# Another order of all pieces in a fused linear-attention and feed-forward kernel

## The chip, the cores and the metric

The kernel runs on 1 core of one Trainium2 chip. The metric is the device time of the program in microseconds (us), the median of three runs. Beside the timed runs there is one execution taken by the hardware profiler; all rows below are of that one.

## The reference

Two stages. The first is a gated linear attention with 4 batches, 8 heads, 768 tokens, head width 32 and 16 states, in fp32. With `cum` the running sum of `log(a)` in a chunk, per head:

```python
L = np.exp(cum[:, :, :, None] - cum[:, :, None, :]) * causal
y_intra = ((Cc @ Bc.T) * L) @ xc
y_inter = (Cc @ state) * np.exp(cum)
state = decay_full * state + sum_j(Bc[j] * decay_from_j[j] * xc[j])
```

The second takes the 256 numbers of a token (8 heads of 32), normalizes them and adds a feed-forward block of hidden width 1024:

```python
xn = (x - mu) / np.sqrt(var + 1e-06) * g_ln
out = x + np.maximum(xn @ w_ch1, 0.0) @ w_ch2
```

The weights arrive as float64 and the inputs as fp32; the matmuls of the feed-forward block are each done on a rounded upper part and on a rest (names ending in h and l), so that three products stand for one.

## The kernel before

**Tiling.** The 768 tokens are six chunks `t` of 128; a chunk is handled for all 4 batches at once (512 columns). In a chunk the attention runs as: decays (`lr`, `dc`, `du`, `x`), scaled inputs `cs`, `cm`, `bs`, `be`; scores `G` (L394, 64 TensorE instructions); `R` = G times the decay table `WW` (L400, four on VectorE); state products `Z` (L433); `K`, `S`, `sbd`, the state between half chunks; `Vi` (L413), what the state gives, and `V` (L421), what the chunk gives, both into PSUM tiles `yps`; `y` copies them to `y32`. Then `yh`, `yl` split them, `T` (L482) transposes them, `tc`, `st`, `ag`, `rs`, `rc` make the statistics of each token.

**Feed-forward.** `h t m` (L513) makes one eighth of the hidden layer in 6 matmuls of 512 columns; `hh` and `hl` (L518/L520, L524) split it; `o t b` (L531) makes the output of one batch in 24 matmuls of 256 columns, `oc` (L541) does the same in pieces of 12 for chunk 0 as the second weights arrive; `oe` (L546) finishes it and `od` stores it. PSUM has 3 buffers for `h` and `o` (a buffer is free when its `hl` or `oe` is done) and 5 for the attention.

**Weights.** Each 512 KB piece of a weight is loaded (`ld w1 c k`, `ld w2 c`) and turned from float64 to fp32 by `k0`, `k1`, `k2`, `k3`, `kr`, `f` (L195, L200, L209, L214, L220, L225). The first weights are then centred: `wc` (L240) on TensorE for half 1, and `wm`, `wf` (L245, L249) for half 0; `wh` and `wl` (L254, L258) split them.

**Order.** There is no scheduler at work: the string `ISSUE` (L584) lists some 640 pieces, each a name with its arguments, and the loop at L577 issues them as they stand. A suffix gives the engine (`:v` VectorE, `:a` ScalarE, `:p` GpSimd). So each engine's instructions run in the order in which the string names them, and each waits for what it reads. `fill` pieces (L558) are matmuls on zeros that nobody reads. `pc` (L171) is a one-element transfer out of a loaded tile: SyncE's queue, which issues all transfers, stops there until that load has landed. A transfer also waits for the transfer eight before it, since eight semaphores are used in turn.

Of the kernel before, what the change touches and what calls it, by code (L numbers as in the profile page):

```python
# [659 lines left out]
```

## Time and profile before

| | |
|---|---|
| three timed runs | 196.64, 197.25, 197.37 us; median 197.25 us |
| profiled execution, its own time | 198.06 us |
| its span (first to last instruction) | 196.3 us |
| mean granted clock of TensorE | 0.981 |
| busy: TensorE matmul, weight load | 187.3 us (95%), 160.3 us (82%) |
| busy: VectorE, ScalarE, GpSimd | 131.0 us (67%), 67.0 us (34%), 38.3 us (20%) |
| chain that ended last | 89% TensorE |

The profiled execution lies 0.81 us above the median, and 1.76 us of it lie outside the span. The page names engines PE (TensorE matmul), PEld (its weight loads), DVE (VectorE), ACT (ScalarE), POOL (GpSimd) and SP (SyncE). A matmul on fp32 operands that isn't a transpose shows as two matmul and two weight-load instructions, one on the split operands as one of each. "Issue" is idle time for which the profile shows no releaser.

### The profile page before, as it was taken

What the parts mean: (1) busy time and instruction counts of PE and PEld (TensorE: products, weight loads), DVE (VectorE), ACT (ScalarE), POOL (GpSimd) and SP (SyncE); (2) the same over time, 40 slices, a digit from 0 to 9 for tenths busy, and PEclk for the clock granted to TensorE, in tenths of its full rate; (3) what the DMA queues carried; (4) which work ended last, traced back from release to release, by engine and by line L of the source; (5) the groups of instructions that cost most, each with busy time, mean ns of one, the idle gap of its engine ahead of it and who ended that gap; (6) DMA issues with size and microseconds to landing.
All of it is one profiled execution on the core that took longest, in us unless ns stands there. A gap on an engine that the chain in (4) does not pass through costs nothing.

```text
span 196.3 us, 6366 instructions
## 1 busy us (share of the span) xinstructions
PE 187.3 (95%) x2834; PEld 160.3 (82%) x2834; DVE 131.0 (67%) x278; ACT 67.0 (34%) x128; POOL 38.3 (20%) x40
## 2 busy tenths in 40 slices
PE   8785999999999999998999999999999999999993
PEld 3664557788899897998878799988999899998993
DVE  2499558999997899585897662496452791447210
ACT  4474598887234502015123540223102030014100
POOL 0043076904543740006420000000000002000000
PEclk9998599999999999999999999999999999999999
DMA  4896894040655033404000500200020001000024
GB/s 139 310 387 233 306 329 161 5 115 0 212 168 164 0 107 102 116 28 140 27 5 3 165 0 13 70 0 3 27 80 3 3 0 58 0 20 6 28 84 134
DMA packets 11670, 18.43 MB, mean 94 GB/s; under 512 B 2394, under 2 KB 5882, under 8 KB 11642
## 3 DMA queue, kind: packets, MB, share of 16 engines
q1 hardware_dynamic: 11642, 18.02, 27.9%
q8 instruction: 22, 0.36, 0.7%
q14 instruction: 6, 0.05, 0.1%
HBM read 14.74 MB, written 3.28 MB: 92 GB/s over the span
## 4 chain that ended last, share of the span: by engine, by line
PE 89%; DMA 3%; DVE 3%; issue 2%; ACT 1%; SPq 1%
PE ph L513 34%; PE po L531 29%; PE pp L541 6%; PE yps L421 5%; PE yps L413 3%; PE yt L482 3%; DMA raw<-in_w_dram 3%; PE G L394 3%; PE wc L240 3%; PE Z L433 2%; DVE o L546 1%; PE wm L245 1%; SPq L164 1%; DVE WW L382 1%; DVE bs L364 0%
## 5 line engine op out<-in xcount | busy, mean ns | idle before, releaser
L531 PE MATMUL po<-w,hh 128*128 128x256 f32 x320 | 56.9, 280 | 0.0
L513 PE MATMUL ph<-yh,w 128*128 128x512 f32 x192 | 53.8, 401 | 0.5 <-issue 0.5
L531 PEld LDWEIGHTS po<-w,hh 128*128 128x128 f32 x320 | 49.3, 188 | 1.5 <-issue 0.7
L531 PE MATMUL po<-w,hl 128*128 128x256 f32 x160 | 44.7, 279 | 0.6 <-issue 0.6
L513 PEld LDWEIGHTS ph<-yh,w 128*128 128x128 f32 x192 | 34.3, 188 | 7.8 <-issue 1.3
L518 ACT ACTIVATE hh<-ph 128x512 fp32r<-128x512 f32 x32 | 18.8, 598 | 57.7 <-PE ph L513 41.2
L524 DVE SCALAR_TENSOR_TENSOR hl<-ph,hh 128x512 fp32r<-128x512 f32 x48 | 32.4, 681 | 8.5 <-ACT hh L518 8.2
L531 PEld LDWEIGHTS po<-w,hl 128*128 128x128 f32 x160 | 30.1, 188 | 0.0
L513 PE MATMUL ph<-yl,w 128*128 128x512 f32 x96 | 29.8, 391 | 0.0
L546 DVE SCALAR_TENSOR_TENSOR o<-po,rstd,ytok 128x256 f32<-128x256 f32 x20 | 9.5, 480 | 26.5 <-PE po L531 26.3
L513 PEld LDWEIGHTS ph<-yl,w 128*128 128x128 f32 x96 | 18.0, 188 | 4.0
L474 POOL TENSOR_TENSOR yl<-y,yh 128x512 fp32r<-128x512 f32 x5 | 7.1, 1423 | 63.9 <-ACT yh L471 62.0
L400 DVE TENSOR_TENSOR R<-G,WW 128x512 f32<-128x512 f32 x24 | 15.5, 676 | 0.8 <-PE G L394 0.8
L520 DVE TENSOR_SCALAR hh<-ph 128x512 fp32r<-128x512 f32 x16 | 10.9, 684 | 7.1 <-PE ph L513 7.0
L421 PE MATMUL yps<-R,xt 64*32 64x64 f32 x768 | 9.8, 239 | 1.8 <-issue 1.8
L541 PE MATMUL pp<-w,hh 128*128 128x256 f32 x64 | 11.4, 280 | 0.0
L421 PEld LDWEIGHTS yps<-R,xt 64*32 64x32 f32 x768 | 8.6, 111 | 2.6 <-issue 2.3
L541 PEld LDWEIGHTS pp<-w,hh 128*128 128x128 f32 x64 | 10.0, 188 | 0.3
L465 ACT COPY y<-yps 128x256 f32<-128x256 f32 x13 | 4.6, 374 | 16.5 <-PE yps L421 10.1
L494 DVE BATCH_NORM_STATS2 st<-ytok 128x6 f32<-128x256 f32 x24 | 9.8, 411 | 0.0
L541 PE MATMUL pp<-w,hl 128*128 128x256 f32 x32 | 8.9, 279 | 0.0
L441 POOL TENSOR_TENSOR K<-S,emt 128x256 f32<-128x256 f32 x6 | 3.8, 639 | 24.2 <-DVE S L449 24.2
(97 smaller groups left out, 229.7 us busy)
## 6 DMA issues: line engine op xcount, KB each, us to landing
raw<-in_w_dram SPq DMA_DIRECT2D x8, 512.0 KB, 5.9
xt<-in_x_dram SPq DMA_DIRECT2D x6, 512.0 KB
out_dram<-o SPq DMA_DIRECT2D x24, 128.0 KB, 1.8
ud<-scr SPq DMA_DIRECT2D x8, 256.0 KB
c<-in_cn_dram SPq DMA_DIRECT2D x6, 256.0 KB
b<-in_bn_dram SPq DMA_DIRECT2D x6, 256.0 KB, 2.8
bt<-in_bt_dram SPq DMA_DIRECT2D x6, 256.0 KB, 4.9
cf<-in_sums_dram SPq DMA_DIRECT2D x1, 256.0 KB
```

Source lines behind the costliest of these rows:

```text
L240: nc.tensor.matmul(w, gd[:, k] if j == k else gneg[:, j:j + 1].to_broadcast([P, P]), f32[1, c, j], start=(n == 0), stop=(n == 1))
L400: nc.vector.tensor_tensor(out=R.rearrange("p b i k -> p b (i k)"), in0=tiles.pop(("G", t, q)).rearrange("p b i k -> p b (i k)"), in1=WW.re ...
L421: nc.tensor.matmul(tiles["y", t, g, f][32 * k:32 * k + 32, b], x[r, b * NH + h], tiles["R", t, h // 2][r, b, h % 2], start=(t + f + b == 0 ...
L474: e.tensor_tensor(out=tiles["yl", t][:, g], in0=tiles["y32", t][:, g], in1=tiles["yh", t][:, g].bitcast(F32), op=ALU.subtract)
L494: nc.vector.bn_stats(out=st, in_=tiles["ytok", t][:, b])
L513: nc.tensor.matmul(ph, W1[m // 4, k][:, s, mc], v[:, k], start=(i == 0), stop=(i == len(cmb) - 1))
L518: e.activation(h, tiles["ph", t, m], AF.Relu)
L520: e.tensor_scalar(out=h, in0=tiles["ph", t, m], scalar1=0.0, scalar2=None, op0=ALU.max)
L524: nc.vector.scalar_tensor_tensor(out=l, in0=tiles.pop(("ph", t, m)), scalar=0.0, in1=tiles["hh", t, m].bitcast(F32), op0=ALU.max, op1=ALU. ...
L531: nc.tensor.matmul(po, tiles[v, t, m][:, cols], W2[m // 2,][:, s, (m % 2) * DM:(m % 2 + 1) * DM], start=(n == 0), stop=(n == len(cmb) - 1))
L541: nc.tensor.matmul(tiles["po", t, b], tiles[v, t, m][:, cols], W2[m // 2,][:, s, (m % 2) * DM:(m % 2 + 1) * DM], start=(c + n + b % 2 == 0 ...
L546: nc.vector.scalar_tensor_tensor(out=o, in0=tiles.pop(("po", t, b)), scalar=tiles["rstd", t][:, b], in1=tiles["ytok", t][:, b], op0=ALU.mu ...
```

## The change

Only the string `ISSUE` is another one. The pieces are the same but for these: the engine of 74 of the pieces differs (a net of eight products move from GpSimd to VectorE: GpSimd's tensor products go from 34 to 26, VectorE's from 67 to 75), the nine `fill` pieces have other widths, and two `pc` pieces stand where five stood. The order is new from the first piece to the last. Two lines of the diff:

```diff
-fill 0 512, ld la, ld sums, ld mask, ld c 0, fill 1 512, ld w1 1 1, l1, ini, l2, lr 0, dc 0, ld id, ones:v, ld b 0, e 1, ld sel, du 0 0, fill 2 128,
+az, fill 0 512, ld la, inv, ld sums, ld mask, ld as, fill 1 512, ld b 0, l1, ini, ld id, l2, ld c 0, lr 0, ld bt 0, ones, fill 2 256, ld sel, rcl,
```

SyncE's queue, after the first three loads, before the change (`raw_116` and `raw_140` are the weight pieces w1 1 1 and w1 1 0; `c`, `b`, `bt`, `xt` are the inputs of chunk 0, `as` the decays of later chunks):

```order
L149 DMA c_113<-in_cn_dram 128x512
L154 DMA raw_116<-in_w_dram 128x1024
L164 DMA cst<-in_consts_dram 128x192
L149 DMA b_131<-in_bn_dram 128x512
L164 DMA selt<-in_sel_dram 32x132
L154 DMA raw_140<-in_w_dram 128x1024
L149 DMA bt_147<-in_bt_dram 128x512
L149 DMA xt_156<-in_x_dram 128x1024
L134 DMA as<-in_as_dram 128x128
```

and after it (`raw_139` is w1 1 0, `raw_146` is w1 1 1; `seen` is a `pc`):

```order
L134 DMA as<-in_as_dram 128x128
L149 DMA b_119<-in_bn_dram 128x512
L164 DMA cst<-in_consts_dram 128x192
L149 DMA c_126<-in_cn_dram 128x512
L149 DMA bt_130<-in_bt_dram 128x512
L164 DMA selt<-in_sel_dram 32x132
L164 DMA gt<-in_g_dram 128x2
L154 DMA raw_139<-in_w_dram 128x1024
L154 DMA raw_146<-in_w_dram 128x1024
L149 DMA xt_148<-in_x_dram 128x1024
L171 DMA seen<-raw_139 1x1
```

The inputs of chunk 0 now stand ahead of both weight pieces, with `xt` behind them, and the queue stops at `seen` until w1 1 0 has landed.

VectorE at its start, before, from the decay table's first half to the first two `R` (`top_159` and `top_187` are the two weight pieces):

```order
L188 COPY WW<-cst 128x32x32
L360 SCALAR_TENSOR_TENSOR cm_145<-c_113,cst,ud_137 128x512 x2
L200 TENSOR_SCALAR top_159<-top_159 128x512
L382 TENSOR_TENSOR WW<-wt,cst 128x32x32
L364 TENSOR_TENSOR bs_185<-b_131,ud_137 128x512
L209 TENSOR_SCALAR top_159<-top_159 128x512
L345 TENSOR_TENSOR cs_226<-c_113,ud_137 128x512
L373 TENSOR_TENSOR be_230<-bt_147,pend 128x512
L200 TENSOR_SCALAR top_187<-top_187 128x512
L214 SCALAR_TENSOR_TENSOR top_159<-raw_116,top_159 128x512
L400 TENSOR_TENSOR R_272<-G_190,WW 128x512
```

and after, from `bs` of chunk 0:

```order
L332 SCALAR_TENSOR_TENSOR uds<-AZs,ini 128x128
L364 TENSOR_TENSOR bs_157<-b_119,ud_151 128x512
L360 SCALAR_TENSOR_TENSOR cm_169<-c_126,cst,ud_151 128x512 x2
L382 TENSOR_TENSOR WW<-wt,cst 128x32x32
L373 TENSOR_TENSOR be_220<-bt_130,pend 128x512
L200 TENSOR_SCALAR top_218<-top_218 128x512
L400 TENSOR_TENSOR R_234<-G_184,WW 128x512
L400 TENSOR_TENSOR R_243<-G_181,WW 128x512
L400 TENSOR_TENSOR R_251<-G_183,WW 128x512
L335 RECIPROCAL inv<-uds 128x4
L400 TENSOR_TENSOR R_278<-G_182,WW 128x512
L200 TENSOR_SCALAR top_275<-top_275 128x512
```

The weight steps no longer stand among what the scores need; three of the four `R` stand ahead of the second weight piece.

TensorE at the end of `V` of chunk 2, before (the last `V` instruction and what follows):

```order
L421 MATMUL yps_995<-R_963,xt_445 32x64
L421 MATMUL yps_996<-R_963,xt_445 32x64
L513 MATMUL ph_1104<-yh_800,w_551 128x512
L513 MATMUL ph_1104<-yh_800,w_544 128x512
L513 MATMUL ph_1104<-yh_800,w_551 128x512
L513 MATMUL ph_1104<-yh_800,w_544 128x512
L513 MATMUL ph_1104<-yl_801,w_551 128x512
L513 MATMUL ph_1104<-yl_801,w_544 128x512
L541 MATMUL pp_1127<-w_867,hh_842 128x256 x2
```

and after:

```order
L421 MATMUL yps_1014<-R_917,xt_439 32x64
L421 MATMUL yps_1015<-R_917,xt_439 32x64
L541 MATMUL pp_1126<-w_871,hh_818 128x256 x2
L541 MATMUL pp_1126<-w_871,hl_880 128x256
L541 MATMUL pp_1126<-w_871,hh_700 128x256 x2
```

Where a part of the hidden layer (`ph`, six matmuls of 512 columns) followed on the 64 products of `V`, now the output pieces of chunk 0 (`pp`) follow.

## Rows read from the trace of the kernel before

**Rows 1.** Page: busy tenths, 40 slices of 4.9 us; TensorE, VectorE, granted clock.

```profile
PE   8785999999999999998999999999999999999993
...
DVE  2499558999997899585897662496452791447210
...
PEclk9998599999999999999999999999999999999999
```

**Rows 2.** Stretches of 5 us: engines' busy us (instructions), granted clock, DMA share, GB/s.

```profile
0.00:5.00 5.00, 4.22 (x11) 2.01 (x12) 1.15 (x4) 2.28 (x3) 0.20 (x4) 1.00 0.52 145
5.00:10.00 5.00, 3.89 (x33) 3.06 (x32) 2.16 (x4) 2.25 (x6) 0.18 (x1) 1.00 0.88 309
10.00:15.00 5.00, 4.38 (x126) 3.23 (x128) 5.00 (x9) 3.79 (x11) 2.10 (x4) 1.00 1.04 387
15.00:20.00 5.00, 3.01 (x167) 2.51 (x159) 4.44 (x11) 2.22 (x7) 1.34 (x2) 0.80 0.69 234
20.00:25.00 5.00, 5.00 (x51) 2.37 (x39) 3.30 (x8) 3.06 (x8) 0.00 (x0) 0.52 0.88 313
```

**Rows 3.** Chain that ended last: start us, duration us, engine and line.

```profile
2.59 5.95 DMA raw<-in_w_dram
...
11.70 1.21 PE G L394 x63
...
14.82 0.69 ACT sbd L457 x2
...
16.90 1.77 issue
18.67 2.03 PE yps L421 x114
20.70 5.68 PE wc L240 x8
...
28.20 1.72 PE wm L245 x4
29.92 4.11 PE ph L513 x18
...
193.11 0.48 DVE o L546
```

**Rows 4.** Timeline of TensorE: start us, us, operation, count, [idle before].

```profile
88.23 1.48 PE L421 MATMUL yps<-R,xt 64*32 64x64 f32 x128
...
91.80 0.28 PE L531 MATMUL po<-w,hl 128*128 128x256 f32 x1 [0.56 <-issue]
...
105.81 1.48 PE L421 MATMUL yps<-R,xt 64*32 64x64 f32 x128
...
108.81 0.63 PE L513 MATMUL ph<-yh,w 128*128 128x512 f32 x2 [0.46 <-issue]
```

**Rows 5.** Page, code packets; then stretches from 0, PE and PEld instructions in brackets.

```profile
q8 instruction: 22, 0.36, 0.7%
...
0.00:16.90 16.90, 14.18 (x221) 9.49 (x221) 10.18 (x20) 10.19 (x24) 3.83 (x9) 1.00 0.82 288
...
0.00:91.30 91.30, 86.50 (x1622) 69.62 (x1623) 71.97 (x149) 44.84 (x89) 32.66 (x35) 0.96 0.48 158
0.00:108.40 108.40, 103.04 (x2004) 83.32 (x2005) 86.91 (x181) 50.64 (x97) 37.00 (x39) 0.97 0.43 139
```

**Rows 6.** Stretch of 36 us where two engines are full, columns as in 2.

```profile
30.00:66.00 36.00, 36.00 (x735) 30.83 (x734) 34.47 (x70) 23.03 (x41) 16.92 (x16) 1.00 0.34 109
```

**Rows 7.** Timeline of POOL: start us, us, operation, [idle before and releaser].

```profile
9.82 1.28 POOL L310 TENSOR_TENSOR mblk<-msum,selt 32x144 f32<-32x144 f32 x1 [9.38 <-DMA selt<-in_sel_dram]
...
14.07 1.05 POOL L368 TENSOR_TENSOR c<-cs,em 128x512 f32<-128x512 f32 x1 [2.90 <-ACT em L323]
```

**Rows 8.** Groups by line: busy us, mean ns of one, idle before.

```profile
L258 DVE TENSOR_TENSOR w<-top,w 128x512 fp32r<-128x512 f32 x3 | 3.1, 1049 | 0.9 <-ACT w L254 0.9
...
L373 DVE TENSOR_TENSOR be<-bt,pend 128x512 f32<-128x512 f32 x3 | 2.0, 681 | 0.0
```

More of the change, by code (lines that the diff above doesn't have):

```diff
@@ new lines @@
+ld g, ru, fill 3 64, ld w1 1 0, dc 0, ld w1 1 1, ld x 0, fill 4 256, du 0 1, e 1, du 0 0, B:v 0, fill 5 256, lr 1, so, cx 0 0, x 1, fill 6 256,
+cx 0 1, e 0, x 0, W:v 0, gm:a, G 0, pc 4 w1 1 0, k0 1 1 0, be:v 0, dc 1, ld w1 0 1, sm, k1 1 1 0, ld w1 0 0, mb, R 0 3, fill 7 512, du 1 0, ld bt 1,
+C 0, R 0 0, ld x 1, kr 1 1 0, sp, R 0 2, em 0, em 1, c2:p 0, Z 0 0, k0 1 1 1, riv, R 0 1, Z 0 1, S 0 0, k1 1 1 1, fill 8 256, sb:a 0 1, k2 1 1 0,
+k2 1 1 1, kr 1 1 1, Vi 0, k3 1 1 1, du 1 1, V 0 0, k3 1 1 0, k0 1 0 1, V 0 1, f:v 1 1 1, y 0 0 0, f:v 1 1 0, wc 1 1, y 0 1 0, kr 1 0 0, k1 1 0 1,
@@ new lines @@
+ld c 2, ro 0, ld c 1, ld b 1, pc 2 w1 0 0, ld w2 0, k2 1 0 1, k0 1 0 0, k3 1 0 1, wc 1 0, be:v 1, k1 1 0 0, ld bt 2, k2 1 0 0, ld w2 2, rd, k3 1 0 0,
+ro 1, ld w2 1, f:v 1 0 0, ld x 2, K 0 1, ld b 2, C:v 1, ld ud 2, wh 1 1 1, kr 1 0 1, y 0 0 1, f 1 0 1, y 0 1 1, wh 1 1 0, T 0 1, yh:a 0 0, Z 1,
+yh:a 0 1, T 0 0, tc 0 1, yl 0 0, wm 0, W 1, wl:v 1 1 0, yl 0 1, S 0 1, wl:v 1 1 1, h 0 5, tc 0 0, K:p 1 0, wf 0 1, cm 1 1, B:v 1, h 0 4, cm 1 0,
+S 1 0, wf 0 0, k0 2 0, sb:v 1 1, G 1, hh 0 4, wh:v 1 0 1, wh 1 0 0, wl:v 1 0 1, hh 0 5, h 0 7, hl 0 4, wl 1 0 0, kr 2 0, hl 0 5, k0 2 2, R 1 0,
@@ new lines @@
+h 0 3, sb 1 0, hh 0 7, R 1 2, c2:p 1, R 1 1, h 0 2, hh 0 3, K:p 1 1, hl 0 7, kr 2 1, B 2, st 0 1, S 1 1, h 0 1, R 1 3, C:v 2, k1 2 0, Vi 1, hh 0 1,
+st 0 2, cm:v 2 0, W 2, hl 0 1, V 1 0, c2 2, V 1 1, hl 0 3, h 0 0, y 1 0 1, ld x 4, k2 2 0, hh 0 2, ld w2 3, k3 2 0, y 1 0 0, ld c 3, y 1 1 1, cm 2 1,
+h 0 6, f:v 2 0, ld bt 3, yh:a 1 0, k1 2 2, K 2 0, y 1 1 0, yl:v 1 0, hh 0 0, G 2, yh:a 1 1, hl 0 2, hh 0 6, st 0 0, T 1 0, yl 1 1, R 2 3, wh 2 0,
+h 1 2, hl 0 0, be 2, hl 0 6, h 1 4, ag 0 0, R 2 2, sb 2 0, ld bt 4, wl:v 2 0, ld ud 3, T 1 1, k2 2 2, h 1 0, R 2 1, tc 1 1, kr 2 2, st 0 3, k3 2 2,
@@ new lines @@
+k0 2 1, oc 0 0 1, ag 0 3, ag 0 1, hh 1 4, k1 2 1, hh 1 0, hl 1 4, tc 1 0, Z 2, k2 2 1, h 1 6, S 2 0, hl 1 0, K:p 2 1, f 2 2, S 2 1, h 1 7, R 2 0,
+sb:v 2 1, k3 2 1, Vi 2, st 1 1, f 2 1, st 1 0, V 2 1, V 2 0, wh:v 2 1, y 2 1 0, be:v 3, oc 0 0 0, wl:v 2 1, ag 0 2, C:v 3, rs 0, y 2 1 1, oc 0 1 1,
+wh 2 2, hh:v 1 7, ld c 4, kr 2 3, ld b 4, wl:v 2 2, ld x 3, k0 2 3, oc 0 1 0, yh 2 1, ld b 3, hh:v 1 6, y 2 0 0, yl 2 1, ld ud 4, y:v 2 0 1, ag 1 0,
+oc 0 2 0, st 1 2, hh 1 2, k1 2 3, sb:a 3 0, hl 1 6, W 3, K 3 0, oc 0 2 1, k2 2 3, hl 1 2, ag 1 2, k3 2 3, h 1 3, B:v 3, f:v 2 3, ld ud 5, h 1 1,
@@ new lines @@
+ag 1 1, hl 1 7, wh 2 3, hh 1 3, wl:v 2 3, h 1 5, hh 1 1, cm 3 1, hl 1 1, yh:a 2 0, oc 0 3 0, rc 0, hl 1 3, hh 1 5, yl 2 0, oe 0 0, cm 3 0, oc 0 3 1,
+c2 3, C:v 4, T 2 0, oe 0 1, h 2 6, c2:p 4, oe 0 2, od 0 1, st 1 3, od 0 2, ld c 5, hh:v 2 6, ld bt 5, ag 1 3, ld b 5, hl 1 5, o 1 0, rs 1, cm 4 1,
+be:v 4, oe 0 3, tc:v 2 0, G 3, R 3 0, T 2 1, o 1 1, rc 1, st 2 1, hl 2 6, tc:v 2 1, R 3 1, R 3 3, Z 3, o 1 3, S 3 0, R 3 2, sb:a 3 1, st 2 3, B:v 4,
+oe 1 1, K 3 1, cm:v 4 0, Vi 3, ag 2 1, S 3 1, V 3 1, V 3 0, y:v 3 1 1, oe 1 0, h 2 3, st 2 0, W:v 4, h 2 0, y:v 3 0 0, y:v 3 0 1, oe 1 3, y:v 3 1 0,
@@ new lines @@
+G 4, od 1 3, st 2 2, yh:a 3 1, ag 2 2, hh 2 3, T 3 1, hl 2 3, o 1 2, R 4 3, R 4 2, C:v 5, R 4 1, c2:p 5, h 2 1, hh 2 0, hl 2 0, R 4 0, Z 4, hh 2 1,
+K 4 0, sb:a 4 0, h 2 5, S 4 0, hl 2 1, K:p 4 1, oe 1 2, T 3 0, sb:v 4 1, tc 3 1, h 2 4, yh 3 0, W:v 5, h 2 2, st 3 2, hh 2 4, tc:v 3 0, yl:v 3 0,
+Vi 4, hh 2 2, hl 2 4, hh:v 2 5, V 4 0, ag 3 2, ag 2 3, hl 2 5, V 4 1, be:v 5, yl:v 3 1, h 3 2, hl 2 2, h 3 5, hh:v 3 2, y:v 4 0 0, ag 2 0, hl 3 2,
+rs 2, h 2 7, hh 3 5, y:v 4 1 1, rc 2, y:v 4 1 0, cm:v 5 0, h 3 0, yh:a 4 1, hl 3 5, hh:v 2 7, yl:v 4 1, hl 2 7, o 2 0, st 3 0, y:v 4 0 1, o 2 2,
@@ new lines @@
+oe 2 0, st 3 1, od 2 0, cm:v 5 1, od 1 2, yh 4 0, ld x 5, S 4 1, ag 3 1, yl:v 4 0, od 0 0, od 1 1, K:p 5 0, o 2 3, B 5, G 5, oe 2 3, sb:v 5 0, Z 5,
+R 5 0, o 2 1, R 5 3, S 5 0, oe 2 2, sb:a 5 1, R 5 1, od 2 2, od 2 3, od 1 0, h 3 3, hh 3 0, hl 3 0, R 5 2, Vi 5, hh 3 3, hl 3 3, T 4 0, oe 2 1,
+h 3 7, h 4 2, hh 3 7, hl 3 7, h 3 1, hh 4 2, hl 4 2, h 3 6, h 4 6, hh:v 3 6, hl 3 6, V 5 0, tc:v 4 0, hh 4 6, hh 3 1, ag 3 0, V 5 1, st 4 0, ag 4 0,
+hl 3 1, h 3 4, hh 3 4, hl 3 4, o 3 1, st 3 3, hl 4 6, ag 3 3, T 4 1, o 3 0, tc 4 1, rs 3, y 5 1 0, rc 3, y 5 1 1, oe 3 1, yh:a 5 1, od 3 1, h 4 1,
@@ new lines @@
+oe 3 0, st 4 3, st 4 1, y:v 5 0 0, o 3 2, o 3 3, oe 3 2, h 4 4, hh 4 1, oe 3 3, yl:v 5 1, od 3 3, od 2 1, hl 4 1, h 4 3, hh 4 4, y 5 0 1, h 4 0,
+hh:v 4 3, hl 4 4, T 5 1, hh:v 4 0, h 4 5, tc 5 1, hl 4 3, yh 5 0, hl 4 0, h 4 7, yl 5 0, hh 4 5, hl 4 5, h 5 1, hh:v 4 7, ag 4 3, st 4 2, ag 4 2,
+h 5 2, ag 4 1, hl 4 7, rs 4, rc 4, o 4 3, hh:v 5 2, hl 5 2, o 4 0, oe 4 3, od 4 3, pc 3 c 1, o 4 2, oe 4 0, od 4 0, T 5 0, o 4 1, tc:v 5 0, st 5 1,
+oe 4 2, hh:v 5 1, hl 5 1, h 5 3, oe 4 1, od 4 1, h 5 0, hh 5 3, hl 5 3, h 5 4, hh 5 0, hl 5 0, h 5 6, hh:v 5 4, hl 5 4, h 5 7, ag 5 1, hh:v 5 6,
@@ L620 @@
+hl 5 6, h 5 5, st 5 2, st 5 0, st 5 3, hh:v 5 7, hh 5 5, ag 5 2, hl 5 7, hl 5 5, o 5 2, ag 5 0, ag 5 3, rs 5, rc 5, o 5 1, o 5 3, oe 5 1, od 5 1,
+od 4 2, od 3 0, o 5 0, oe 5 3, oe 5 2, od 5 3, od 3 2, od 0 3, od 5 2, oe 5 0, od 5 0
 """
```

34 lines of the change are left out of this document (removed).

## The prediction

> **What bounds the kernel now.** I read the slices first [rows 1]: TensorE is busy in 99% of nearly every slice from the fifth on, VectorE only in the first ten or twelve. So from about 20 us on the time is TensorE's work laid end to end, and that work is the same in both kernels: no matmul is added or taken away but the idle `fill` ones, all of which lie in the start. What an order can change is (a) when the first `h` begins, (b) stops of TensorE after it, (c) the tail. The chain of waits gives (a): the first `h` begins at 29.92 and the last output follows at 193.11 [rows 3]; 163.2 us lie between, in which TensorE stands idle for little over 1 us.
>
> What holds up the first `h` is in the same chain, read backwards: `wm` 1.72, two transposes and `Z` (1.8 together), `wc` 5.68, `V` 2.03 plus a stop of 1.77 us marked "issue", and before that the state of chunk 0 (`sbd` at 14.82). Two things in it are not work. First the clock: the granted clock is 0.80 in 15 to 20 us and 0.52 in 20 to 25 [rows 2], so TensorE runs at its lower level, 1.2 GHz instead of 2.4, right after a stretch in which it did 64-column products and then stood still. `wc` is eight instructions of the form of which `wm` has four: at the full clock it takes 2 x 1.72 = 3.44 us, not 5.68; and `V` takes 1.48 us at the full clock [rows 4], not 2.03 for 114 of its 128.
>
> Second the stop itself. It has no releaser, and there are two smaller ones like it, 0.56 us at 91.80 and 0.46 us at 108.81 [rows 4]. Counting TensorE's instructions up to each [rows 5]: 442, 3245, 4009. The distances, 2803 and 764, are 11 and 3 times 254.8. And the page has 22 code packets for 5668 shown instructions, 258 each. I take it that code comes in blocks of about 255 shown instructions, that a block is asked for when the one ahead is begun, and that TensorE stops where it runs through a block faster than the next one comes. How long that takes I read at the stops: block 13 begins 24 instructions into the `V` that starts at 88.23, so at 88.3, and work goes on at 91.80, 3.5 us later; block 16 begins at 105.9, and work goes on at 108.81, 2.9 us later. The first stop is the loaded case: the count says that the block ahead begins halfway through `G` (11.70 to 12.9), at 12.3, and work goes on at 18.67, 6.4 us later, with the DMA queue moving 387 GB/s meanwhile [rows 2, 3].
>
> The Trainium skill ("Runtime: NRT & Kernel Launch", Instruction fetch mechanics) says that code is refilled in blocks of 256 instructions, as counted here, that TensorE holds 2048 of them, and that crossing a border is mostly hidden. Three stops on borders speak against the last two.
>
> **The change part by part, up to `V` of chunk 0.** Loads: the first weight piece lands at 8.55 [rows 3], when the loads up to it make 1.16 MB and the rates of [rows 2] give 1.8 MB moved, so 0.4 to 0.65 MB of later loads are under way beside. In the new queue `b` stands at 0.71 MB, `c` at 1.07, `bt` at 1.32, w1 1 0 at 1.85, w1 1 1 at 2.36, `x` at 2.87. With that excess and those rates `c` lands at about 7.8, w1 1 0 at 10.4, w1 1 1 at 11.8; `x` at 12.3 to 13.4, since `seen` holds back what would run beside it. VectorE does `cm` (two of 0.7) by 9.4, and `G` runs from 9.5 instead of 11.70. That is not what ends last, though. `Vi` of chunk 0 needs the table `em`, made by ScalarE's first weight step, `msum`, GpSimd's `mblk` (1.28) and the spread on TensorE, and then c2 on GpSimd [rows 7]; before, that chain began at the weight's landing at 8.55 but `mblk` waited for `sel` till 9.82. Now it begins at 10.4: `msum` 11.2, `mblk` to 12.6, a moved `cs` (1.28) behind it on GpSimd to 13.9, c2 to 14.9. `Z`, `S` and `sbd` end at 15.4, as `x` lands no earlier. So `Vi` starts at 15.5, before at 15.6: no gain.
>
> The gain comes behind it. Block 2 is now asked for at 10.4, with about 1.0 MB of loads ahead instead of some 1.8 MB, and is wanted at 16.4: 6.0 us, against 6.4 under the heavier load. I take no stop (bounds 0 and 0.4). `V` ends at 17.9 instead of 20.70: 1.77 us of stop, the rest the clock. VectorE's weight steps end at 17.9 as well, eleven steps of 0.3 to 0.7 us after `be`, so `wc` starts at once and at the full clock saves 5.68 - 3.44 = 2.24. That makes 5.0 us.
>
> Against it: block 3 is then asked for at 16.4 and wanted at 20.5, within `wc`, 4.1 us later. Bounds are 2.9 (no stop) and 6.4 (stop of 2.3); some 1.3 MB of loads are ahead of it (both half-0 weights, `bt`, `x`, `c`, `b`), which at 350 GB/s is 3.7 us before the packet and 5.5 in all: 1.4 us of stop. `wc` ends at 22.7; the two transposes with `Z` (1.8) and `wm` (1.72) end at 26.3, as in the old order. Beside them ScalarE's `wh` and two `yh` (0.6 each) and GpSimd's two `yl` (1.25 each) run to 26.7, but only the last of the six matmuls of `h` reads the second `yl`, 1.1 us after the first. So the first `h` starts at 26.3 instead of 29.92: **-3.6 us** (bounds -5.0 and -2.7).
>
> **After the first `h`.** The borders counted along the new order: block 13 now takes 4.0 us (two `h` stand in it) and block 16 2.9, so the stops of 0.56 and 0.46 go, **-1.0**, save 0.1 for block 16 (bounds 0 and 0.6). A new short one is block 9: it holds 234 instructions of `V` of chunk 2 and, where an `h` stood, 22 of `pp` behind it: 1.3 + 1.3 = 2.6 us, against 2.9 to 3.5 needed: **+0.5** (bounds 0.3 and 0.9, and 3.8 if the load of 6.4 us were to meet it).
>
> VectorE: eight products come over from GpSimd at 0.68 (`be`) to 1.05 us (`wl`) [rows 8], with other swaps a net of some 4 us on 131. They cost nothing where VectorE has slack, but from 30 to 66 us it is busy for 34.5 of 36 us and TensorE for all 36 [rows 6]: there VectorE sets when PSUM comes free. Summing its instructions along the new order from `wf` to the `hl` of part 6 of chunk 1 gives 68 of them, 32.6 us, against 35.3 us of TensorE's work up to the `h` that waits for it; before it was 72 and 35.6. The tightest place is `hl 0 0`: 33 instructions, 17.3 us, against 17.6. So it just keeps up; for slips of tenths I put **+0.3** (bounds 0 and 1.5, what VectorE had idle in those 36 us). The tail (last `o`, `oe`, store) has the same length.
>
> Sum: -3.6 - 1.0 + 0.1 + 0.5 + 0.3 = -3.7 us. On the profiled 198.06 that is 194.3; it was 0.81 above the median, so on the median 197.25 - 3.7 = **193.5 us**.
>
> **Rivals.** *The clock falls again* (0.22). `Z`, `Vi` and `V` of chunk 0 still stand in a row from 13.1 to 17.9 with 0.6 us of idling among them, and after such a stretch it fell before [rows 2]. For: the same small products. Against: the long stop is gone and two wider fills stand there. Price: 0.55 for `V` and 2.24 for `wc`, less up to 1.4, as slower `wc` hides the stop at block 3: +1.4 to +2.8, so 194.9 to 196.3.
>
> *VectorE becomes the bound from 26 to 65 us* (0.18), the rival on the slow side. TensorE comes 3.6 us earlier, and VectorE can't follow if its instructions wait for ScalarE's `hh` in the new order or cost more than in these rows (`wl` has cost 1049 ns where `be`, of the same size, cost 681 [rows 8]). Carried on to the `hl` of part 7 of chunk 1 the sum is 36.6 us against 38.0 of TensorE's, so an excess f on VectorE's side holds TensorE for f x 36.6 - 1.4 us: 10% gives 2.3, 20% gives 5.9, so 195.8 to 199.4. It decides from 14%, where the whole gain of 3.7 is gone.
>
> *The stops aren't code* (0.05), as the skill's sizes would have it. Then the stop in `V` stays (1.77), as do the later two (1.0), and block 3, 9 and 16 cost nothing (-2.0): 193.5 + 0.8 = 194.3.
>
> **How the numbers follow.** Forecast 0.55, at 193.5 (192 to 195 for its own bounds); clock 0.22; VectorE 0.18; not code 0.05. About 0.5%, 1 us, is what a measurement of this kernel tells from no change, so faster means under 196.3 and slower over 198.2. Faster: 0.54 + 0.14 + 0.03 + 0.05 = 0.76. Same: 0.01 + 0.06 + 0.07 = 0.14. Slower: 0.02 + 0.08 = 0.10. The range runs from 191.9, no stop at block 3, to 196.6, which takes in the clock and the cheaper half of VectorE.
>
> **What would show it.** Right: no "issue" of 1.8 us in `V` of chunk 0; `V` done near 18; granted clock 1.00 from 15 to 25; an "issue" of about 1.4 us in `wc`; the first `ph` near 26.3; an "issue" of half a microsecond after `V` of chunk 2, none near 91 and 108. Wrong: a clock of 0.5 in 15 to 25, or TensorE waiting for `hl` or `R` between 30 and 65.

## The result

The changed kernel takes 195.95 us (median of 17 executions, 193.82 to 198.05) against 197.39 us for the kernel before in the same sessions (17 executions, 196.17 to 198.25): a ratio of 0.989, 95% interval 0.9861 to 0.9918. The ratio takes only the executions within 1.5% of the quickest of their kernel, which leaves out the six longest of the changed kernel and none of the kernel before, so it flatters the change: 1.1%, 2.2 us by the ratio, but 0.7%, 1.44 us by the medians of all 17. The forecast was 193.5 us, and 195.95 lies inside its range.

The two profiled executions tell another story: 198.06 us before, 194.59 us after, spans 196.3 and 192.6, so -3.7 us of span, which is the forecast sum to the tenth. But that execution is the fourth quickest of the 17. What the other executions lose against it is what had to be found.

Page of the changed kernel: busy tenths in 40 slices of 4.8 us, and the code packets.

```profile
PE   8989799999999899999999999999999999999993
...
DVE  1699999999889687868899955636433772359321
...
PEclk9999999999999999999999999999999999999999
...
q8 instruction: 22, 0.36, 0.8%
```

Against [rows 1], the clock row has no dip, TensorE's slices up to the tenth are as full as before, VectorE's are fuller, and the code comes in as many packets. The same stretches as in [rows 2] and [rows 6] (length, then busy us and instructions of PE, PEld, DVE, ACT, POOL; granted clock, DMA share, GB/s):

```profile
15.00:20.00 5.00, 4.71 (x167) 3.15 (x167) 4.90 (x11) 4.09 (x10) 0.00 (x0) 1.00 0.98 349
20.00:25.00 5.00, 3.64 (x77) 2.15 (x76) 4.93 (x10) 3.52 (x9) 2.43 (x2) 1.00 0.87 295
30.00:66.00 36.00, 35.43 (x683) 30.02 (x670) 32.96 (x71) 21.84 (x41) 12.11 (x12) 1.00 0.39 129
```

The clock is 1.00 where it was 0.80 and 0.52. The chain that ended last, to be held against [rows 3]:

```profile
17.50 3.20 PE wc L240 x7
20.70 1.36 issue
22.06 0.70 PE wc L240
...
24.57 1.72 PE wm L245 x4
26.29 2.77 PE ph L513 x12
...
58.25 6.14 DMA b<-in_bn_dram
66.43 1.66 PE ph L513 x6
```

The stop of 1.77 us in `V` is gone, a stop of 1.36 us stands in `wc` instead, and the first `ph` begins at 26.29 instead of 29.92. New is the row at 58.25: a load of `b` is part of the chain. The timeline shows who waits for it (start, duration, what; in brackets the idle time before and its releaser), with the other stop of TensorE:

```profile
57.30 0.28 PE L541 MATMUL pp<-w,hl 128*128 128x256 f32 x1 [0.47 <-issue]
66.43 1.20 PE L513 MATMUL ph<-yh,w 128*128 128x512 f32 x4 [0.53 <-DVE hl L524]
...
64.41 0.69 DVE L364 TENSOR_TENSOR bs<-b,ud 128x512 f32<-128x512 f32 x1 [1.55 <-DMA b<-in_bn_dram]
...
56.91 0.33 SPq L149 DMA_DIRECT2D c<-in_cn_dram  x1
57.29 0.42 SPq L149 DMA_DIRECT2D b<-in_bn_dram  x1
57.81 0.39 SPq L149 DMA_DIRECT2D xt<-in_x_dram  x1
58.25 0.42 SPq L149 DMA_DIRECT2D b<-in_bn_dram  x1
```

SyncE stands until VectorE has read the `c` whose buffer `c` of chunk 4 takes (that product ends at 56.88), and then issues four loads in a row. VectorE needs the last of them first: `b` of chunk 3. It lands at 58.25 + 6.14 = 64.39; VectorE has waited 1.55 us for it, the `hl` behind it comes late, and TensorE waits 0.53 us for that.

Two instructions show the other thing that had not been forecast:

```profile
21.12 1.69 DVE L214 SCALAR_TENSOR_TENSOR top<-raw,top 128x512 int32<-128x512 int32 x1
...
20.86 1.40 POOL L225 TENSOR_TENSOR top<-top,low 128x512 int32<-128x512 int32 x1 [6.42 <-ACT low L220]
```

This instruction of VectorE takes 0.65 to 0.69 us everywhere else in this trace; here it begins 0.26 us into a product of GpSimd and takes 1.0 us more.

### The profile page after: what moved, and what is told of

Read it like the earlier page. It is cut to its first block, busy times and chain, and to the rows that moved or that the text cites. A ratio compares the mean times of both kernels' runs of the same rounds, so it can differ in the third digit from the quotient of the medians.

```text
span 192.6 us, 6374 instructions
## 1 busy us (share of the span) xinstructions
PE 185.3 (96%) x2834; PEld 159.2 (83%) x2834; DVE 134.3 (70%) x282; ACT 67.4 (35%) x132; POOL 27.8 (14%) x32
## 4 chain that ended last, share of the span: by engine, by line
PE 82%; DMA 7%; DVE 4%; SPq 3%; issue 2%; POOL 1%; POOLq 0%
PE ph L513 32%; PE po L531 29%; PE yps L421 4%; DMA xt<-in_x_dram 4%; DMA b<-in_bn_dram 3%; PE yt L482 3%; PE G L394 3%; PE yps L413 3%; PE Z L433 2%; PE pp L541 2%; PE wc L240 2%; SPq L164 1%; SPq L149 1%; PE wm L245 1%; POOL top L225 1%
## 5 line engine op out<-in xcount | busy, mean ns | idle before, releaser
L524 DVE SCALAR_TENSOR_TENSOR hl<-ph,hh 128x512 fp32r<-128x512 f32 x48 | 32.5, 680 | 9.9 <-ACT hh L518 9.6
L518 ACT ACTIVATE hh<-ph 128x512 fp32r<-128x512 f32 x33 | 19.4, 597 | 49.4 <-PE ph L513 42.5
L546 DVE SCALAR_TENSOR_TENSOR o<-po,rstd,ytok 128x256 f32<-128x256 f32 x20 | 9.5, 480 | 21.7 <-PE po L531 21.6
L474 POOL TENSOR_TENSOR yl<-y,yh 128x512 fp32r<-128x512 f32 x6 | 8.1, 1351 | 59.7 <-DVE yh L471 37.9
L400 DVE TENSOR_TENSOR R<-G,WW 128x512 f32<-128x512 f32 x24 | 15.7, 678 | 1.1 <-PE G L394 1.1
L520 DVE TENSOR_SCALAR hh<-ph 128x512 fp32r<-128x512 f32 x15 | 10.3, 684 | 3.9 <-PE ph L513 3.8
L457 ACT ACTIVATE sbd<-S,cst 128x128 f32<-128x128 f32 x10 | 3.5, 393 | 19.0 <-DVE S L449 19.0
L494 DVE BATCH_NORM_STATS2 st<-ytok 128x6 f32<-128x256 f32 x24 | 9.6, 413 | 0.0
L558 PE MATMUL idle<-const-float32-0.0 128*128 128x256 f32 (+2 forms) x18 | 8.6, 601 | 0.8 <-PEq L648 0.8
L421 PE MATMUL yps<-R,xt 64*32 64x64 f32 x768 | 8.9, 225 | 0.0
L421 PEld LDWEIGHTS yps<-R,xt 64*32 64x32 f32 x768 | 7.9, 105 | 0.7 <-issue 0.4
```

The costliest lines, as they stand in the source:

```text
L400: nc.vector.tensor_tensor(out=R.rearrange("p b i k -> p b (i k)"), in0=tiles.pop(("G", t, q)).rearrange("p b i k -> p b (i k)"), in1=WW.re ...
L421: nc.tensor.matmul(tiles["y", t, g, f][32 * k:32 * k + 32, b], x[r, b * NH + h], tiles["R", t, h // 2][r, b, h % 2], start=(t + f + b == 0 ...
L474: e.tensor_tensor(out=tiles["yl", t][:, g], in0=tiles["y32", t][:, g], in1=tiles["yh", t][:, g].bitcast(F32), op=ALU.subtract)
L494: nc.vector.bn_stats(out=st, in_=tiles["ytok", t][:, b])
L518: e.activation(h, tiles["ph", t, m], AF.Relu)
L520: e.tensor_scalar(out=h, in0=tiles["ph", t, m], scalar1=0.0, scalar2=None, op0=ALU.max)
```

## The experiments

**Once more the same.** The changed kernel was profiled twice more, first to see what repeats.

> The changed kernel unaltered, another execution of it. Its 17 timed runs lie between 193.82 and 198.05 us, and the profiled one (194.59) was among the quick ones. Theory A (the start varies: loads, code blocks and the clock there): the first h begins anywhere between 25.5 and 29 us, and from the first h to the last output it takes the same 162.6 us within 0.5. Theory B (VectorE's full stretch varies): the first h begins near 26.3 in this execution too, and the stretch from 30 to 66 us holds 1 us or more of TensorE's waits for hl, R or y beyond the 0.5 of the first execution.

195.05 us, span 193.0. Up to the first `ph` (26.27) everything repeats within 0.1 us, the stop in `wc` with 1.32 us too. TensorE waits 0.99 us for `hl` near 66 us instead of 0.53. The other one came later:

> The changed kernel once more, unchanged, to see what differs between its executions. If the landing of b 3 is what spreads them, VectorE's wait for it and TensorE's wait for hl near 66 us go with the time: about 0.5 us of TensorE's wait in a run of 192.6 us span, 1.4 us in one of 194 us. If a collision on VectorE between 17 and 30 us spreads them, the first ph moves by up to 1 us with it. If the clock does, a stretch of about 7 us at half of it shows.

197.37 us, span 195.3, clock 1.00 up to 190 us: one of the longer executions. Its timeline:

```profile
27.86 1.33 PE L513 MATMUL ph<-yh,w 128*128 128x512 f32 x4 [1.79 <-DVE w L258]
59.20 0.28 PE L541 MATMUL pp<-w,hl 128*128 128x256 f32 x1 [0.49 <-issue]
69.12 1.19 PE L513 MATMUL ph<-yh,w 128*128 128x512 f32 x4 [1.28 <-DVE hl L524]
...
21.61 1.70 DVE L214 SCALAR_TENSOR_TENSOR top<-raw,top 128x512 int32<-128x512 int32 x1
...
23.95 1.49 DVE L441 TENSOR_TENSOR K<-S,emt 128x256 f32<-128x256 f32 x1
25.36 1.75 DVE L345 TENSOR_TENSOR cs<-c,ud 128x512 f32<-128x512 f32 x1
27.04 0.68 DVE L258 TENSOR_TENSOR w<-wc,w 128x512 fp32r<-128x512 f32 x1
...
23.45 3.12 POOL L474 TENSOR_TENSOR yl<-y,yh 128x512 fp32r<-128x512 f32 x2 [0.70 <-ACT yh L471]
```

Three of VectorE's instructions take 1.0 to 1.1 us too long (0.68, 0.42 and 0.68 are their usual times), each begun within GpSimd's `f` or one of its two `yl`. `wl` (L258) ends 2.65 us later than in the quick execution (27.72 against 25.07), and the first `ph` begins at 27.86, 1.57 us later, although `wm` was done at 26.07. Near 66 us TensorE waits 1.28 us. From the first `ph` to TensorE's last instruction it is 164.1 us against 162.9. By the ends of the first four `ph` matmuls (29.19 against 27.22) the first place costs 1.97 us and the second 0.75 more than in the quick execution; these two make up the 2.7 us between the two spans.

**The hold, the fills, one load.** Three parts of the forecast, undone one at a time.

```diff
-G 0, pc 4 w1 1 0, k0 1 1 0, be:v 0, dc 1,
+G 0, k0 1 1 0, be:v 0, dc 1,
```

> The changed order without the first pc, which stops SyncE's queue until w1 1 0 has landed. Half-0 weights and what follows are issued some 3 us earlier, so about 1.5 MB more stand ahead of the code block asked for at 10.2 us and of x. Theory A: x of chunk 0 lands later than 13.4 (14 to 15), the packet of block 2 starts after 14 instead of 12.9, V of chunk 0 shows a stop of up to 1.5 us, while block 3's stop in wc (1.36) shrinks since its loads are done earlier; in all the first h 0 to 2 us later, time +0 to +2. If the hold does nothing (rival), x, both stops and the time stay as they are within 0.3 us.

197.12 us (10 executions), ratio to before 0.9955, interval 0.9917 to 0.9993: most of the gain is gone. The clock fell in nine of the ten executions (a mean of 0.972 to 0.991). In the profiled execution, one of the longest (200.09 us), `xt` of chunk 0 lands some 3 us later; `Z` begins at 16.32 instead of 13.49 and the first `ph` at 30.83. But there `w1 1 0` came late as well (TensorE waits 2.90 us for `mblk`, which stands behind that piece's first step on ScalarE), and the execution had three of the long VectorE instructions, so the size stayed open until the run without them, below.

```diff
-ld bt 0, ones, fill 2 256, ld sel,
+ld bt 0, ones, fill 2 128, ld sel,
...
-mb, R 0 3, fill 7 512, du 1 0,
+mb, R 0 3, fill 7 256, du 1 0,
...
-S 0 0, k1 1 1 1, fill 8 256,
+S 0 0, k1 1 1 1, fill 8 128,
```

> The changed order with the three fills at the old widths (128, 256 and 128 columns instead of 256, 512 and 256). Theory that the wider fills hold the clock: in most executions the granted clock drops to half between 15 and 25 us, as in the kernel before (mean clock 0.98 instead of 1.00), V and wc are up to 2.8 us longer and the time is 1.4 to 2.8 us longer. Rival, that the clock held because the long stop in V is gone: the clock stays at 1.00 in most executions and the time is the same within 0.3 us.

196.5 us (10 executions), ratio 0.9958, interval 0.9919 to 0.9996. The granted clock was 0.995 or more over the span in 3 of 10 executions, against 12 of 17 of the changed kernel and none of the 25 of before beside it. So the clock fell more often with the narrow fills (in a later run, below, it held with them in four of five executions, so the fills don't decide it alone). This kernel takes 0.55 us more than the changed one by the medians (1.3 by the ratios), not the 1.4 to 2.8 us expected, and its seven executions with a fall are no longer than the three without (means of 196.43 and 196.53 us). Here is the profiled execution, a stretch and the timeline (its last row is the first `ph`):

```profile
15.00:20.00 5.00, 4.82 (x164) 3.61 (x165) 4.78 (x10) 3.62 (x8) 0.00 (x0) 0.66 0.90 329
...
18.02 1.56 PE L240 MATMUL wc<-top,gd 128*128 128x512 f32 x2
...
21.13 1.17 PE L240 MATMUL wc<-top,gneg 128*128 128x512 f32 x2
...
26.21 1.33 PE L513 MATMUL ph<-yh,w 128*128 128x512 f32 x4 [0.35 <-DVE w L258]
```

`V` and the start of `wc` run at half clock, `wc` begins 0.6 us later, and the stop of 1.36 us in it is nearly gone (the last pair of `wc` takes 1.17 us, undisturbed ones 1.02): the code packet arrives when it arrives. The first `ph` begins at 26.21, no later than at the full clock.

```diff
-ld c 2, ro 0, ld c 1, ld b 1,
+ro 0, ld c 1, ld b 1,
...
-ld x 2, K 0 1, ld b 2, C:v 1,
+ld x 2, K 0 1, ld b 2, ld c 2, C:v 1,
```

> The changed order with the load of c of chunk 2 (256 KB) put behind the loads of x and b of chunk 2, so that it is not ahead of the code block that is asked for at 16.05 us. If that packet waits for the loads issued before it: its start falls from 19.8 to about 19.1, the stop in wc from 1.36 to 0.6 or 0.7, the first h from 26.3 to 25.6. If the code packet's delay has another cause, stop and first h stay within 0.2 us.

196.3 us (10 executions), ratio 0.9923, interval 0.9876 to 0.9971: not told apart from the changed kernel. The stop in `wc` shrank to 0.90 us, less than expected, but the first `ph` began at 26.94, 0.54 us after a wait for `wl`, behind two long VectorE instructions (L338 1.49, L345 1.76).

**The late load.**

```diff
-h 0 6, f:v 2 0, ld bt 3, yh:a 1 0,
+h 0 6, f:v 2 0, ld bt 3, ld b 3, yh:a 1 0,
...
-ld x 3, k0 2 3, oc 0 1 0, yh 2 1, ld b 3, hh:v 1 6,
+ld x 3, k0 2 3, oc 0 1 0, yh 2 1, hh:v 1 6,
```

> The changed kernel with the load of b for tile 3 issued right behind bt 3 (about 40.2 us) instead of last of four behind c 4 (58.25 us). In the changed kernel it lands at 64.39 us, VectorE stands 1.55 us at the product bs that reads it (64.41 us), the next hl comes late, and TensorE waits 0.53 us at 66.43 us; in the other executions traced so far VectorE stands 1.5 to 2.2 us there and TensorE 0.8 to 1.4 us. Theory 'a late load starves VectorE': VectorE does not wait for b any more, TensorE's wait for hl near 66 us falls below 0.2 us, from the first ph to TensorE's end it is 162.0 to 162.5 us instead of 162.9 to 164.4, the median falls by 0.5 to 1.2 us against the changed kernel (195.95 us), and the spread of the executions narrows, since the landing varies. Rival 'VectorE's own work is the bound there', as predicted: VectorE fills the time it gains with work that was due anyway, TensorE still waits 0.4 us or more for hl, and the median moves by less than 0.3 us.

194.9 us (6 executions, 193.64 to 195.58), ratio 0.9853, interval 0.9807 to 0.9899: 1.05 us better than the changed kernel by the medians, as expected, and 0.4% by the ratios, whose intervals overlap. The timeline of its profiled execution:

```profile
41.86 0.44 SPq L149 DMA_DIRECT2D b<-in_bn_dram  x1
...
63.74 0.65 DVE L214 SCALAR_TENSOR_TENSOR top<-raw,top 128x512 int32<-128x512 int32 x1
64.32 0.68 DVE L364 TENSOR_TENSOR bs<-b,ud 128x512 f32<-128x512 f32 x1
...
27.51 1.33 PE L513 MATMUL ph<-yh,w 128*128 128x512 f32 x4 [1.79 <-DVE w L258]
```

`bs` now follows at once, and no wait of TensorE for `hl` is left between 30 and 165 us; from the first `ph` to TensorE's end it is 162.7 us, a little over the 162.0 to 162.5 expected. So VectorE's own work does not set the time there. The spread remains, and the profiled execution shows why: three long VectorE instructions again, and the first `ph` at 27.51.

**Do VectorE and GpSimd exclude each other?** Seven products more on GpSimd, on a scratch tile that nobody reads, where GpSimd was idle:

```diff
+    def busy(i):
+        nc.gpsimd.tensor_tensor(out=junk, in0=junk, in1=junk, op=ALU.mult)
...
-kr 2 1, B 2, st 0 1,
+kr 2 1, B 2, bu 0, bu 1, bu 2, bu 3, st 0 1,
...
-R 2 2, sb 2 0, ld bt 4,
+R 2 2, sb 2 0, bu 4, bu 5, bu 6, ld bt 4,
```

> The changed kernel with seven products on GpSimd more (128x512 f32, a scratch tile by itself, nothing reads it): four behind bs of tile 2 (about 35.3 to 40.5 us) and three behind sbd of tile 2 (about 45.4 to 49.3 us), where GpSimd is idle in the changed kernel for 7.3 and 5.0 us. Theory 'the engines exclude each other': a VectorE instruction whose operands are both tensors in SBUF does not run while GpSimd runs such a product, so the ones at L345, L368, L214, L225, L441, L474, L258 in these stretches take up to 1.1 us longer each (0.68 to as much as 1.78 us); VectorE loses 2 to 4 us in all between 35 and 50 us, TensorE waits for VectorE there or near 66 us by 1 to 3 us, and the time rises by 1 to 3 us. Rival 'no link': GpSimd's products delay nothing on VectorE, its instructions keep their 0.42 and 0.68 us, and the time stays within 0.5 us of the changed kernel.

203.21 us (4 executions), ratio 1.0213, interval 1.0141 to 1.0286: 5.7 us slower than before by the medians (4.2 by the ratio) and 7.3 us slower than the changed kernel, for work that no one waits for. Timeline and one stretch:

```profile
35.46 1.58 DVE L345 TENSOR_TENSOR cs<-c,ud 128x512 f32<-128x512 f32 x1
36.96 1.26 DVE L200 TENSOR_SCALAR top<-top 128x512 f32<-128x512 f32 x1
38.14 0.41 DVE L494 BATCH_NORM_STATS2 st<-ytok 128x6 f32<-128x256 f32 x1
38.48 0.92 DVE L355 TENSOR_SCALAR cm<-cs,cst 128x512 f32<-128x512 f32 x1
39.32 0.68 DVE L524 SCALAR_TENSOR_TENSOR hl<-ph,hh 128x512 fp32r<-128x512 f32 x1
...
35.44 4.85 POOL L572 TENSOR_TENSOR junk<-junk 128x512 f32<-128x512 f32 x4
...
40.05 1.20 PE L513 MATMUL ph<-yh,w 128*128 128x512 f32 x4 [1.44 <-DVE hl L524]
...
47.54 2.07 PE L513 MATMUL ph<-yh,w 128*128 128x512 f32 x4 [2.67 <-DVE hl L524]
...
45.00:50.00 5.00, 2.46 (x6) 1.97 (x7) 5.00 (x9) 0.00 (x0) 4.84 (x5) 0.68 0.45 151
```

While GpSimd works, the products and scalings of VectorE on tensors in SBUF take 0.45 to 0.9 us longer; `st` (0.41) and `hl` (0.68), which reads PSUM, take what they always take. TensorE waits 1.44 and 2.67 us, and within the second wait its clock falls (0.68 in 45 to 50 us). These waits alone exceed the 1 to 3 us expected, and the fall comes on top.

Over the ten traces taken up to this run, I counted VectorE's instructions that begin at least 0.1 us into a GpSimd product with at least 0.45 us of it still to come, and called long what exceeds its line's usual time by over 0.25 us:

| begun inside a GpSimd product | long |
|---|---|
| two tensors in SBUF: L214, L225, L258 (on `top`), L338, L345, L382, L441, L459, L474 | 22 of 22 |
| one tensor in SBUF, scaled at 0.42 to 0.47 us for 512 columns: L200, L355 | 3 of 3 |
| an operand in PSUM: L249, L258 (on `wc`), L400, L449, L465, L520, L524, L546 | 0 of 159 |
| one tensor in SBUF, no such scaling: L335, L494, L497 | 0 of 52 |

The Trainium skill ("SBUF — State Buffer", Who interferes with whom) has the rule: VectorE and GpSimd share one pair of ports as an exclusive lock; an instruction of VectorE with two inputs in SBUF, or in one of its two-port modes, is blocked until GpSimd's is done, and whoever begins first wins. The rows agree to about a tenth: the long instruction of the changed kernel would have begun its usual 0.68 us at 21.12 + 1.69 - 0.68 = 22.13, and GpSimd's product ends at 20.86 + 1.40 = 22.26.

**The products out of GpSimd's hands,** with the load of `b` moved as above:

```diff
-y 0 0 1, f 1 0 1, y 0 1 1,
+y 0 0 1, f:v 1 0 1, y 0 1 1,
...
-tc 0 1, yl 0 0, wm 0,
+tc 0 1, yl:v 0 0, wm 0,
...
-wl:v 1 1 0, yl 0 1, S 0 1,
+wl:v 1 1 0, yl:v 0 1, S 0 1,
```

> The load of b 3 moved ahead as in the run before it, and the three GpSimd products between 20.9 and 26.9 us (f 1 0 1, 1.40 us; yl 0 0 and yl 0 1, 2.88 us together) put on VectorE (0.68 us each, 2.0 us more work for it there). Theory 'the engines exclude each other': no VectorE instruction between 17 and 28 us takes over 1.2 us any more (in the executions traced so far one or two of them take 1.07 us too long, at another place each time), which gives back 1.0 to 2.1 of the 2.0 us; the first ph stays within 0.4 us of 26.3 us, and the time is within 0.6 us of the kernel that only moves the load. Rival 'no link': long instructions stay, VectorE is 2 us later at wl and hl, the first ph comes at 27 us or later, TensorE waits 1 us or more for hl between 27 and 40 us, and the time rises by 1 to 2 us.

193.91 us (4 executions, 193.76 to 194.23), ratio 0.9825, interval 0.9785 to 0.9864: the four executions lie within 0.5 us, and both kernels are beaten. From the timeline:

```profile
27.71 0.50 PE L513 MATMUL ph<-yh,w 128*128 128x512 f32 x1 [0.41 <-DVE w L258]
```

VectorE has 2.0 us more to do, none of its instructions is long by over 0.25 us, and TensorE waits 0.41 us within the first `h`, for `wl`, less than the 1.55 to 1.79 us that it lost in the executions with three collisions. By the medians it is 1.0 us below the kernel that only moves the load, better than expected; by the ratios it is 0.55 us, and the intervals overlap. So the traces show that the collisions are gone; what time this gives back is known no better than by these two numbers.

The products alone (the diff above by itself), the load left where it was:

> The changed kernel with only the three GpSimd products between 20.9 and 26.9 us put on VectorE; the load of b 3 stays last of four. If the two causes are separate: no VectorE instruction between 17 and 28 us takes over 1.2 us, the first ph near 26.3 us, executions close together; VectorE still stands 1.5 to 2.4 us for b 3 and TensorE 0.5 to 1.4 us for hl near 66 us; median 194.4 to 195.0 us, that is 0.5 to 1.0 us above the kernel that has both (193.91 us) and 1.0 to 1.5 us below the changed kernel. Rival (the load is all, the move only costs VectorE time): median at or above the changed kernel's 195.95 us.

195.13 us (6 executions), ratio 0.9896, interval 0.9863 to 0.9929. It is 1.2 us above the kernel with both edits, as the first theory had it; that it would be 1.0 to 1.5 us below the changed kernel was too much (0.8 by the medians, 0.6 with each median held against that of the kernel before beside it, nothing by the ratios). Nor did the executions lie close together: 194.51 to 197.89 us. The profiled execution, the longest of the six, shows what the late load can cost:

```profile
66.37 0.69 DVE L364 TENSOR_TENSOR bs<-b,ud 128x512 f32<-128x512 f32 x1 [2.95 <-DMA b<-in_bn_dram]
...
68.39 1.74 PE L513 MATMUL ph<-yh,w 128*128 128x512 f32 x4 [1.89 <-DVE hl L524]
...
70.00:75.00 5.00, 5.00 (x33) 4.77 (x32) 2.60 (x7) 1.68 (x3) 1.27 (x1) 0.78 0.12 48
```

VectorE waits 2.95 us, TensorE 1.89, both more than expected, and the clock falls behind that wait. A late load pays twice here.

**Hold, fills and the one load again, with both causes out.** These are the three edits from above, each on top of the kernel with the load early and the products on VectorE. Without the hold:

> Both causes out, and the hold of SP's loads behind w1 1 0 taken out again, so that the eight loads behind it are issued from 6.8 us on. The profile of the run without the hold had x 0 land 3 us later and the first ph at 30.83 us instead of 26.3, but also three collisions of 1.07 us. If the hold is worth what the landing of x 0 says: Z at 15.5 to 16.5 us instead of 13.8, first ph at 28.5 to 29.5 us, median 196.0 to 197.0 us. Rival (most of that run's loss was the collisions): first ph before 27.5 us and median under 195 us.

195.47 us (6 executions), ratio 0.9888, interval 0.985 to 0.9926: without the hold it is 1.6 us slower. From its timeline, and a stretch:

```profile
15.15 1.32 PE L433 MATMUL Z<-xt,be 64*32 64x64 f32 x64 [2.25 <-DMA xt<-in_x_dram]
...
15.00:20.00 5.00, 4.85 (x199) 3.94 (x203) 4.25 (x9) 2.84 (x7) 0.00 (x0) 0.56 0.96 342
```

Against the kernel with the hold, `Z` begins at 15.15 instead of 13.77 (TensorE waits 2.25 us for `xt`), the clock then falls to 0.56 in 15 to 20 us, which costs `Z` to `V` another 1.5, and `wc` gets 0.6 back since its stop is gone: `wm` ends at 28.93 instead of 26.60. `Z` came a little under the lower bound of the first theory, the first `ph` (28.93) within its bounds, the median 0.5 us under. The hold is worth 1.2 us (by the ratios) to 1.6 us (by the medians), and the changed kernel with and without it had differed by 1.2 us in their medians. The 4.5 us by which the first `ph` came later in the first profile without it belong to that execution: 1.55 us of them are a wait for `wl` behind the collisions, and part of the rest is the late landing of `w1 1 0`, which this profile doesn't have.

With the narrow fills:

> Both causes out, and the three widened fills back to half their columns. If they hold TensorE's clock and the clock is worth what rows show: the granted clock falls to half for 3.4 to 6.8 us from about 15 us on in most executions (0.98 to 0.99 over the span), V and wc run at half speed for that long, but up to 1.4 us of it lies under the stop at TensorE's third block, so 0.3 to 2 us more: median 194.2 to 195.9 us. Rival (the clock is covered by that stop altogether): within 0.2 us of 193.91 us, although the clock falls.

193.71 us (5 executions, 193.40 to 194.11), ratio 0.9822, interval 0.9794 to 0.985: the same as with the wide fills. But the clock fell in one of the five only (a mean of 0.991; 0.997 or more in the others), not in most, so the median says little about the price of a fall. The profiled execution is that one; a stretch, and the timeline of `wc`'s last pair and of `h`:

```profile
15.00:20.00 5.00, 4.77 (x164) 3.67 (x165) 4.47 (x9) 3.62 (x8) 0.00 (x0) 0.69 0.94 313
...
20.91 1.40 PE L240 MATMUL wc<-top,gneg 128*128 128x512 f32 x2
...
26.77 0.50 PE L513 MATMUL ph<-yh,w 128*128 128x512 f32 x1 [0.24 <-DVE w L258]
```

The clock did fall (0.69), `wc` began 0.5 us later, and the stop took that up: 0.4 us of it is left (1.40 us for a pair that takes 1.02 without it). It is the quickest of the five (193.40 us). So the rival holds for this execution, as it did for the first one with narrow fills: a fall here costs nothing as long as the third block's packet ends `wc`. In the run without the hold, where that stop was gone, it did cost time.

With `c 2` loaded later:

> Both causes out (products on VectorE, b 3 early), and the load of c 2 behind those of x 2 and b 2 as well. The packet of TensorE's third block then stands behind one load less: alone, that took its stop in wc from 1.36 to 0.9 us, but its first ph came late for a collision on VectorE. If the collision hid the gain there: stop 0.8 to 1.0 us, first ph 0.3 to 0.5 us earlier than in the kernel without it (26.27 us), median 193.3 to 193.7 us. Rival (the stop is not what the first ph waits for, VectorE's wl is): first ph and median unchanged within 0.2 us.

194.16 us (6 executions, 192.96 to 194.91), ratio 0.9836, interval 0.9801 to 0.987: no gain, and executions that lie 1.95 us apart though both causes are out. In the profiled execution the clock fell for 3.41 us and `Z` had waited 1.08 us for VectorE's `R`, so `V` ended late (19.33) and the third block's packet came only at 20.76 us. Whether one load less ahead of the packet shortens the way to `h` stays open.

## Why the prediction was right, and where not

**Code blocks: right.** No stop in `V` of chunk 0; 1.36 us in `wc` (forecast 1.4); 0.47 after `V` of chunk 2 (0.5); none near 91 us, and none at block 16, where 0.1 was put. In every trace with that stop work goes on 2.2 to 2.4 us after the third block's packet begins (19.79 to 22.06 in the changed kernel, 19.93 to 22.37 in the best one). The rival that these stops are not code is out: a stop moved to each border that the count named. Counted as in [rows 5], 442 shown instructions of TensorE stand ahead of the stop in `V` before the change, 698 ahead of the one in `wc` after it (256 more), and 2223 ahead of the one at 57.30. That 1.36 meets 1.4 so closely is in part luck: the block took 6.0 us from its request at 16.05 where 5.5 was booked (of that, the 1.8 us behind the packet's start rest on no row; they are the 2.2 to 2.4 above), and it was wanted after 4.65 us, not 4.1.

**First `h`: right in sum, in the quick execution, with one term that two traces show to be worth nothing.** 26.29 against 26.3, with two slips of 0.4 us that cancel: `V` ended at 17.50, not 17.9, and `wc` at the full clock took 3.9 us without its stop (3.20 and 0.70), not 3.44. And I booked 2.24 us for `wc` at the full clock and then 1.4 back for the stop at block 3, and priced the clock's fall at +1.4 to +2.8 us. The two profiled executions with the old fills and a fall give about nothing (194.88 and 193.40 us, each the quickest of its run): the price was taken from a `wc` mostly at half clock, as in [rows 3], while in them a fall lasts 3.41 us and ends before `wc` or in its first pair (18.1 and 18.9 us), and what it delays lies under the stop. What a fall costs in other executions stays open: of the 17 of the changed kernel the five with one are 1.3 us longer on average (196.8 against 195.5), and no trace shows where they had it. The wait for the packet is the later of two ends; the two may not be added. What carries the gain, as far as the runs go, is that inputs and the second block come sooner: the hold alone is worth 1.2 to 1.6 us, and the packet of the second block begins at 12.93 instead of 16.50. What the order of the loads and that of VectorE's first steps are worth by themselves, no run took apart.

**VectorE: the step that failed.** "So it just keeps up; for slips of tenths I put +0.3." The sum was right (the 68 instructions up to that `hl` are busy for 33.1 us; 32.6 forecast), and the rival with VectorE's work as the bound falls with the early load, which removes TensorE's wait altogether. The size was wrong, because a sum of durations holds neither of two things. The first is a wait: a load four deep in a queue that stood behind a buffer, 1.55 to 2.95 us of VectorE, 0.53 to 1.89 us of TensorE. I had followed the loads only up to the first `h`. The second is the exclusion: 1.0 to 1.1 us for each collision, one to three of them between 20 and 29 us, and up to 1.8 us at the first `h`. The sign of it was in [rows 8]: a `wl` of 1049 ns where `be` costs 681. I read a mean of three as a price; in the trace of before it is one instruction of 1.78 us, begun 0.36 us into a product of GpSimd:

```profile
65.43 1.78 DVE L258 TENSOR_TENSOR w<-top,w 128x512 fp32r<-128x512 f32 x1
...
65.07 1.59 POOL L474 TENSOR_TENSOR yl<-y,yh 128x512 fp32r<-128x512 f32 x1 [3.68 <-ACT yh L471]
```

That the change moves eight products from GpSimd to VectorE made me look for more work on VectorE; which products were left on GpSimd beside a full VectorE was the question to ask.

**The predicted time: 2.45 us too low.** The -3.7 us were taken off the median. They belong to an execution without much bad luck: with the load early and no collisions the median is 193.91 us, 0.4 from the forecast; the two causes cost the typical execution the other 2.0 us (1.3 by the ratios). That 195.95 lies within the range of 191.9 to 196.6 is luck in part: its upper end was made of the clock and of VectorE's work, and neither is what cost the 2.0 us. No execution of the kernel before was without a fall of the clock (a mean of 0.979 to 0.991 in the 47 executions beside the experiments), so its spread said little about the new kernel's.

## What to carry to other kernels

Where a busy engine just keeps up, don't only sum its work: go through its queue for the loads it will meet, with what stands ahead of them in the issuing queue, and for products of the engine it shares ports with. A mean that is half as large again as its kind is a mixture: look at the single instructions before using it as a price. And where two things end at the same place (slow work and a packet), count the later one, not their sum.
